# Loading two 1 KB vectors as rows and spreading one of them with four small matmuls, in place of 256 packets of 8 bytes

## The chip, the cores and the metric

One core of one Trainium2 chip. The metric is device time in microseconds (us). A profiled execution also has a span, some 2 us shorter than that time; all times inside an execution are counted from the start of its span. In the lines of the profiles PE is TensorE (PEld its weight loads), DVE is VectorE, ACT is ScalarE, POOL is GpSimd; SPq and ACTq are the instruction queues of SyncE and ScalarE, q1 is the DMA queue of the big loads and q10 that of x and gate_w.

## The reference

One decode step: a sliding-window attention branch and a gated feed-forward branch, mixed by a scalar gate.

```python
x = A_x                                              # 1 x 1 x 512
g = sigmoid((x * gate_w).sum(-1, keepdims=True))     # gate_w: 512
a = A_ref(x, k_cache, v_cache, wq, wo)               # q = x @ wq; softmax(q k) v; @ wo
b = B_ref(x, w_gate, w_up, w_down)
return g * a + (1 - g) * b
```

The attention reads the last 4096 positions of 8 key and 8 value heads, 1 MB each. With wq, wo and the three feed-forward weights that is 30.67 MB for each run; x and gate_w are 1 KB each.

## The kernel before

All big loads stand in one queue, issued by SyncE (SP) in the order wq (two halves), 8 kn (keys), w_gate, w_up, 8 vv (values), wo (two halves), wd (three pieces). Only x and gate_w come by a second queue, issued by ScalarE (ACT). They land spread over the 128 partitions, 4 elements (8 bytes) on each, as the matmuls need x:

```python
xg = const.tile([P, 2, DC], BF16, name="xg")         # P = 128, DC = 4
nc.scalar.dma_start(xg[:, 0, :], A_x[0, 0, :].rearrange("(p c) -> p c", c=DC))
nc.scalar.dma_start(xg[:, 1, :], gate_w.rearrange("(p c) -> p c", c=DC))
dq = nc.sync
for i in range(2):
    dq.dma_start(wq_sb[:, 2 * i:2 * i + 2, :], wq_v[:, 2 * i:2 * i + 2, :])
# ... kn, w_gate, w_up, vv, wo, wd on dq; the gate (z_ps, gg) from xg ...
for k in range(4):
    for c in range(DC):
        for hb in range(2):
            nc.tensor.matmul(q_ps[:, hb, :], lhsT=xg[:, 0, c:c + 1].to_broadcast([P, P]), rhs=wq_sb[:, c, ...], ...)
    nc.scalar.copy(q_sb[...], q_ps[...])
    nc.vector.transpose(qtT[...], q_sb[...])
# ... kT = transposes of kn, S_ps = scores, e_sb, pv_ps, o_ps, oY ...
for c in range(NC_O):
    nc.tensor.matmul(a_ps[q0:q0 + 32, :], lhsT=oY[:, c:c + 1].to_broadcast([P, 32]), rhs=wo_sb[:, c, :], ...)
for j in range(N_BULK):
    nc.tensor.matmul(a_ps[q0:q0 + 32, :], lhsT=hT[:, j, :], rhs=wd_sb[:, j, :], ...)
# ... f_ps with the last pieces of wd, res, store ...
```

Of the kernel before, what the change touches and what calls it, by code (L numbers as in the profile page):

```python
# [10 lines left out]
ALU = mybir.AluOpType  # L11
AX = mybir.AxisListType
BF16 = mybir.dt.bfloat16
F32 = mybir.dt.float32
# [3 lines left out]
def kernel(  # L18
# [14 lines left out]
    nc = tc.nc  # L33

    P = 128
    D = A_x.shape[-1]
    DC = D // P
# [20 lines left out]
    const = ctx.enter_context(tc.tile_pool(name="const", bufs=1))  # L58
# [4 lines left out]
    work = ctx.enter_context(tc.tile_pool(name="work", bufs=1))  # L63
    ps_big = ctx.enter_context(tc.tile_pool(name="ps_big", bufs=2, space=bass.MemoryType.PSUM))
    ps_S = ctx.enter_context(tc.tile_pool(name="ps_S", bufs=1, space=bass.MemoryType.PSUM))
    ps_m = ctx.enter_context(tc.tile_pool(name="ps_m", bufs=2, space=bass.MemoryType.PSUM))


    xg = const.tile([P, 2, DC], BF16, name="xg")
    nc.scalar.dma_start(xg[:, 0, :], A_x[0, 0, :].rearrange("(p c) -> p c", c=DC))  # L70
    nc.scalar.dma_start(xg[:, 1, :], gate_w.rearrange("(p c) -> p c", c=DC))

    dq = nc.sync
    wq_sb = big.tile([P, DC, HQ * DH], BF16, name="wq_sb", tag="big")
# [34 lines left out]
    ident = const.tile([P, P], BF16, name="ident")  # L109
# [4 lines left out]
    ones_f = const.tile([P, P], F32, name="ones_f")  # L114
# [7 lines left out]
    nc.vector.tensor_reduce(selI[:], identf[:].rearrange("p (x r) -> p r x", x=4), axis=AX.X, op=ALU.add)  # L122


    gpr = work.tile([P, DC], F32, name="gpr")
    gsum = work.tile([P, 1], F32, name="gsum")
    nc.vector.tensor_tensor(gpr[:], xg[:, 0, :], xg[:, 1, :], op=ALU.mult)  # L127
    nc.vector.tensor_reduce(gsum[:], gpr[:], axis=AX.X, op=ALU.add)  # L128
    z_ps = ps_m.tile([P, 1], F32, name="z_ps", tag="m")
    nc.tensor.matmul(z_ps[:], lhsT=ones_f[:], rhs=gsum[:], start=True, stop=True)  # L130
    gex = work.tile([P, 1], F32, name="gex")
    nc.scalar.activation(gex[:], z_ps[:], AF.Exp, scale=-1.0)
    nc.vector.tensor_scalar_add(gex[:], gex[:], 1.0)
# [7 lines left out]
    for k in range(4):  # L141
        q_ps = ps_big.tile([P, 2, 512], F32, name="q_ps", tag="b")
        for c in range(DC):
            for hb in range(2):
                n0 = k * 1024 + hb * 512
                nc.tensor.matmul(q_ps[:, hb, :], lhsT=xg[:, 0, c:c + 1].to_broadcast([P, P]),  # L146
                                 rhs=wq_sb[:, c, n0:n0 + 512], start=(c == 0), stop=(c == DC - 1))
        nc.scalar.copy(q_sb[:, k * 1024:(k + 1) * 1024], q_ps[:].rearrange("p a b -> p (a b)"))  # L148
        nc.vector.transpose(qtT[:].bitcast(F32)[:, k * 512:(k + 1) * 512],  # L149
                            q_sb[:].bitcast(F32)[:, k * 512:(k + 1) * 512])  # L150
# [13 lines left out]
    for g in range(Hkv):  # L164
# [3 lines left out]
        for dhi in range(2):  # L168
            for t in range(2):
                for hb in range(2):  # L170
                    nc.tensor.matmul(S_ps[:, hb, :], lhsT=q_st[:, g, dhi, :, t],  # L171
                                     rhs=k_v[:, hb * 16:(hb + 1) * 16, dhi, :, t],
                                     start=(g == 0 and dhi == 0 and t == 0),
                                     stop=(g == Hkv - 1 and dhi == 1 and t == 1))
# [11 lines left out]
                     start=True, stop=True)  # L186
# [11 lines left out]
    for c in range(DC):  # L198
        for j in range(4):
            for w, wsb in enumerate((wg_sb, wu_sb)):  # L200
                nc.tensor.matmul(gu_ps[32 * j:32 * j + 32, w, 0:FQ],  # L201
                                 lhsT=xg[:, 0, c:c + 1].to_broadcast([P, 32]),
                                 rhs=wsb[:, c, j * FQ:(j + 1) * FQ], start=(c == 0), stop=(c == DC - 1))


# [25 lines left out]
    for b in range(2):  # L231
        pv_ps = ps_big.tile([P, 4, P], F32, name="pv_ps", tag="b")
        for gq in range(4):
            g = 4 * b + gq
            for m in range(KB // 4):
# [3 lines left out]
                                 lhsT=eT[:, g, 4 * m:4 * m + wj, :].rearrange("p k h -> p (k h)"),  # L239
                                 rhs=vv[g][:, 4 * m:4 * m + 4, :],  # L240
                                 start=(m == 0), stop=(m == KB // 4 - 1), skip_group_check=True)
# [3 lines left out]
        for j in range(4):  # L245
            nc.tensor.matmul(o_ps[:], lhsT=pv_sb[:, j, :], rhs=sel_v[:, j, :, :],  # L246
                             start=(j == 0), stop=(j == 3))
# [11 lines left out]
    for c in range(NC_O):  # L259
        q0 = 32 * (c % 4)  # L260
        nc.tensor.matmul(a_ps[q0:q0 + 32, :], lhsT=oY[:, c:c + 1].to_broadcast([P, 32]),  # L261
                         rhs=wo_sb[:, c, :], start=(c < 4), stop=False, skip_group_check=True)
    for j in range(N_BULK):
        q0 = 32 * (j % 4)
        nc.tensor.matmul(a_ps[q0:q0 + 32, :], lhsT=hT[:, j, :], rhs=wd_sb[:, j, :],  # L265
                         start=False, stop=(j >= N_BULK - 4), skip_group_check=True)
# [14 lines left out]
    for n in range(4):  # L281
        nc.tensor.matmul(f_ps[32 * n:32 * n + 32, :], lhsT=w32[:], rhs=a_sb[:, n * P:(n + 1) * P],  # L282
                         start=False, stop=False, skip_group_check=True)
# [35 lines left out]
```

## Time and profile before

| | before |
|---|---|
| time | 84.33 us (84.29 to 84.5, 3 runs) |
| span of the profiled run | 82.5 us |
| TensorE, VectorE busy | 47.4 us, 34.4 us |
| moved from memory | 30.67 MB |
| packets on the queue of x and gate_w | 288, of which 256 carry 8 bytes |
| x, gate_w: issue to landing | 7.6 us, 12.8 us |

The lines stand in the prediction below. The DMA row of the time strip says how full the transfer engines are; the chain of waits says what ended last, link by link, but not how much slack a link has.

### The profile page before, as it was taken

The numbers are of one execution on the slowest core, as the hardware profiler recorded it, in microseconds if no ns is written. First come the engines' busy times: TensorE is split into PE (matmuls) and PEld (weight loads), VectorE is DVE, ScalarE is ACT, GpSimd is POOL, SyncE is SP. The second block draws the span as 40 slices with busy tenths as digits, with TensorE's granted clock in tenths as the row PEclk, the third lists the DMA queues.
The fourth block names the chain that finished last, engine by engine and source line by source line (L and its number), as shares of the span: only waits on it lengthen the run. The fifth ranks groups of instructions, "written<-read, shape, count | busy, mean of one in ns | idle before, by whom it ended". The sixth has DMA issues, their size and how long they took to land.

```text
span 82.5 us, 734 instructions
## 1 busy us (share of the span) xinstructions
PE 47.4 (58%) x286; PEld 20.8 (25%) x286; DVE 34.4 (42%) x43; ACT 8.9 (11%) x13; POOL 5.0 (6%) x11
## 2 busy tenths in 40 slices
PE   0000000999980059999999213999969955035950
PEld 0000000433420023444443012434354342011420
DVE  0000001300899999999990706219990011000210
ACT  1400000004463000000000060020020020000010
POOL 7970000000000000000000000000000000000000
PEclk9999999999999956999999995558999999555555
DMA  5799899999999999999999999999999999998000
GB/s 103 278 381 429 342 374 405 421 429 425 433 413 425 417 425 436 417 438 445 431 379 417 413 413 433 417 417 421 421 461 397 461 413 429 388 403 314 24 0 1
DMA packets 3898, 30.71 MB, mean 372 GB/s; under 512 B 696, under 2 KB 824, under 8 KB 952
## 3 DMA queue, kind: packets, MB, share of 16 engines
q1 hardware_dynamic: 3608, 30.67, 90.1%
q10 hardware_dynamic: 288, 0.00, 0.2%
q8 instruction: 2, 0.03, 0.2%
HBM read 30.67 MB, written 0.00 MB: 372 GB/s over the span
## 4 chain that ended last, share of the span: by engine, by line
DMA 69%; DVE 14%; PE 9%; ACT 2%; issue 1%; ACTq 0%; DVEq 0%
DMA wd_sb<-in_B_w_down_dram 30%; DMA vv<-in_A_v_cache_dram 23%; DMA xg<-in_gate_w_dram 16%; DVE kT L166 8%; PE q_ps L146 6%; ACT q_sb L148 2%; DVE qtT L149 2%; DVE qbig L158 2%; PE a_ps L265 2%; PE f_ps L282 1%; PE z_ps L130 1%; DVE a_sb L268 1%; ACTq L70 0%; DVE res L287 0%; DVE gpr L127 0%
## 5 line engine op out<-in xcount | busy, mean ns | idle before, releaser
L171 PE MATMUL S_ps<-kT,qbig 128*128 128x512 bf16 x64 | 15.4, 401 | 5.5 <-DVE qbig L158 5.5
L166 DVE STREAM_TRANSPOSE kT<-kn 128x2048 f32<-128x2048 f32 x8 | 17.8, 2276 | 0.0
L238 PE MATMUL pv_ps<-vv,eT 128*16 128x512 bf16 (+1 forms) x64 | 10.2, 408 | 0.0
L171 PEld LDWEIGHTS <-qbig 128*128 128x128 bf16 x64 | 6.4, 101 | 14.4 <-issue 7.8
L146 PE MATMUL q_ps<-wq_sb,xg 128*128 128x512 bf16 x32 | 9.2, 451 | 0.2 <-ACT q_sb L148 0.2
L130 PE MATMUL z_ps<-gsum,ones_f 128*128 128x1 f32 x2 | 0.6, 347 | 14.6 <-DVE gsum L128 14.6
L127 DVE TENSOR_TENSOR gpr<-xg 128x4 f32<-128x4 bf16 x1 | 0.2, 163 | 14.1 <-DMA xg<-in_gate_w_dram 14.1
L238 PEld LDWEIGHTS <-eT 128*16 128x16 bf16 (+1 forms) x64 | 4.1, 97 | 5.5 <-issue 1.9
L261 PE MATMUL a_ps<-wo_sb,oY 128*32 128x512 bf16 x32 | 2.9, 504 | 4.1 <-DMA wo_sb<-in_A_wo_dram 3.8
L146 PEld LDWEIGHTS <-xg 128*128 128x128 bf16 x32 | 3.7, 119 | 5.4 <-issue 3.0
L149 DVE STREAM_TRANSPOSE qtT<-q_sb 128x512 f32<-128x512 f32 x4 | 2.8, 690 | 4.8 <-ACT q_sb L148 4.8
L148 ACT CAST q_sb<-q_ps 128x1024 bf16<-128x1024 f32 x4 | 4.0, 1013 | 6.1 <-PE q_ps L146 6.1
L268 DVE COPY a_sb<-a_ps 128x256 f32<-128x256 f32 x1 | 0.4, 425 | 9.2 <-PE a_ps L265 9.2
L130 PEld LDWEIGHTS z_ps<-gsum,ones_f 128*128 128x128 f32 x2 | 0.5, 310 | 14.5 <-issue 14.5
L120 POOL MEMSET qbig<- 128x4160 bf16 x1 | 3.6, 3567 | 0.0
L201 PE MATMUL gu_ps<-wu_sb,xg 128*32 128x448 bf16 x16 | 3.2, 580 | 0.0
L201 PE MATMUL gu_ps<-wg_sb,xg 128*32 128x448 bf16 x16 | 3.2, 561 | 0.0
L219 DVE RECIPROCAL sg<-sge 128x448 f32<-128x448 f32 x1 | 3.0, 2953 | 0.0
L246 PE MATMUL o_ps<-identf,pv_sb 128*128 128x16 f32 x16 | 2.1, 265 | 1.4 <-ACT pv_sb L243 1.4
L248 DVE TENSOR_TENSOR oT<-o_ps,rb 128x16 bf16<-128x16 f32 x2 | 0.3, 169 | 6.0 <-PE o_ps L246 6.0
L188 ACT ACTIVATE nb<-mb_ps 128x1 f32<-128x1 f32 x1 | 0.2, 171 | 22.5 <-PE mb_ps L185 22.5
L246 PEld LDWEIGHTS o_ps<-identf,pv_sb 128*128 128x128 f32 x16 | 1.9, 191 | 2.4 <-ACT pv_sb L243 2.4
(52 smaller groups left out, 27.3 us busy)
## 6 DMA issues: line engine op xcount, KB each, us to landing
kn<-in_A_k_cache_dram SPq DMA_DIRECT2D x8, 1024.0 KB, 17.9
vv<-in_A_v_cache_dram SPq DMA_DIRECT2D x8, 1024.0 KB, 20.1
wq_sb<-in_A_wq_dram SPq DMA_DIRECT2D x2, 2048.0 KB, 7.5
wo_sb<-in_A_wo_dram SPq DMA_DIRECT2D x2, 2048.0 KB, 24.2
wg_sb<-in_B_w_gate_dram SPq DMA_DIRECT2D x1, 1792.0 KB, 21.7
wu_sb<-in_B_w_up_dram SPq DMA_DIRECT2D x1, 1792.0 KB, 23.6
wd_sb<-in_B_w_down_dram SPq DMA_DIRECT2D x1, 1152.0 KB, 25.1
wd_sb<-in_B_w_down_dram SPq DMA_DIRECT2D x1, 512.0 KB, 23.9
```

The costliest lines, as they stand in the source:

```text
L120: nc.gpsimd.memset(qbig[:], 0.0)
L130: nc.tensor.matmul(z_ps[:], lhsT=ones_f[:], rhs=gsum[:], start=True, stop=True)
L146: nc.tensor.matmul(q_ps[:, hb, :], lhsT=xg[:, 0, c:c + 1].to_broadcast([P, P]), rhs=wq_sb[:, c, n0:n0 + 512], start=(c == 0), stop=(c == D ...
L148: nc.scalar.copy(q_sb[:, k * 1024:(k + 1) * 1024], q_ps[:].rearrange("p a b -> p (a b)"))
L149: nc.vector.transpose(qtT[:].bitcast(F32)[:, k * 512:(k + 1) * 512], q_sb[:].bitcast(F32)[:, k * 512:(k + 1) * 512])
L166: nc.vector.transpose(kT[:].bitcast(F32), kn[g][:].rearrange("p k d -> p (k d)").bitcast(F32))
L171: nc.tensor.matmul(S_ps[:, hb, :], lhsT=q_st[:, g, dhi, :, t], rhs=k_v[:, hb * 16:(hb + 1) * 16, dhi, :, t], start=(g == 0 and dhi == 0 an ...
L201: nc.tensor.matmul(gu_ps[32 * j:32 * j + 32, w, 0:FQ], lhsT=xg[:, 0, c:c + 1].to_broadcast([P, 32]), rhs=wsb[:, c, j * FQ:(j + 1) * FQ], s ...
L219: nc.vector.reciprocal(sg[:], sge[:])
L238: nc.tensor.matmul(pv_ps[32 * gq:32 * gq + mm, :, :], lhsT=eT[:, g, 4 * m:4 * m + wj, :].rearrange("p k h -> p (k h)"), rhs=vv[g][:, 4 * m ...
L246: nc.tensor.matmul(o_ps[:], lhsT=pv_sb[:, j, :], rhs=sel_v[:, j, :, :], start=(j == 0), stop=(j == 3))
L261: nc.tensor.matmul(a_ps[q0:q0 + 32, :], lhsT=oY[:, c:c + 1].to_broadcast([P, 32]), rhs=wo_sb[:, c, :], start=(c < 4), stop=False, skip_gro ...
```

## The change

The intent: the first matmul waited for x and gate_w until 14 us. As one row each on one partition they are one data packet each. TensorE then turns x into a column: four matmuls with one row of x as weights and the number 1 as the moving operand. The gate's sum needs no spreading any more.

```diff
-    xg = const.tile([P, 2, DC], BF16, name="xg")
-    nc.scalar.dma_start(xg[:, 0, :], A_x[0, 0, :].rearrange("(p c) -> p c", c=DC))
-    nc.scalar.dma_start(xg[:, 1, :], gate_w.rearrange("(p c) -> p c", c=DC))
+    xr = const.tile([1, 2, D], BF16, name="xr")
+    nc.scalar.dma_start(xr[:, 0, :], A_x[0, :, :])
+    nc.scalar.dma_start(xr[:, 1, :], gate_w.rearrange("(o n) -> o n", o=1))
@@
-    gpr = work.tile([P, DC], F32, name="gpr")
-    gsum = work.tile([P, 1], F32, name="gsum")
-    nc.vector.tensor_tensor(gpr[:], xg[:, 0, :], xg[:, 1, :], op=ALU.mult)
+    xt_ps = ps_m.tile([P, DC], F32, name="xt_ps", tag="m")
+    for c in range(DC):
+        nc.tensor.matmul(xt_ps[:, c:c + 1], lhsT=xr[:, 0, c:D:DC], rhs=ident[0:1, 0:1],
+                         start=True, stop=True, skip_group_check=True)
+    xT = const.tile([P, DC], BF16, name="xT")
+    nc.vector.tensor_copy(xT[:], xt_ps[:])
+    gpr = work.tile([1, D], F32, name="gpr")
+    gsum = work.tile([1, 1], F32, name="gsum")
+    nc.vector.tensor_tensor(gpr[:], xr[:, 0, :], xr[:, 1, :], op=ALU.mult)
@@
-    nc.tensor.matmul(z_ps[:], lhsT=ones_f[:], rhs=gsum[:], start=True, stop=True)
+    nc.tensor.matmul(z_ps[:], lhsT=ones_f[0:1, :], rhs=gsum[:], start=True, stop=True)
@@ in the q and the feed-forward matmuls
-    lhsT=xg[:, 0, c:c + 1].to_broadcast(...)
+    lhsT=xT[:, c:c + 1].to_broadcast(...)
```

More of the change, by code (lines that the diff above doesn't have):

```diff
@@ L145 @@
                 n0 = k * 1024 + hb * 512
-                nc.tensor.matmul(q_ps[:, hb, :], lhsT=xg[:, 0, c:c + 1].to_broadcast([P, P]),
+                nc.tensor.matmul(q_ps[:, hb, :], lhsT=xT[:, c:c + 1].to_broadcast([P, P]),
                                  rhs=wq_sb[:, c, n0:n0 + 512], start=(c == 0), stop=(c == DC - 1))
@@ L201 @@
                 nc.tensor.matmul(gu_ps[32 * j:32 * j + 32, w, 0:FQ],
-                                 lhsT=xg[:, 0, c:c + 1].to_broadcast([P, 32]),
+                                 lhsT=xT[:, c:c + 1].to_broadcast([P, 32]),
                                  rhs=wsb[:, c, j * FQ:(j + 1) * FQ], start=(c == 0), stop=(c == DC - 1))
```

## The prediction

> **What bounds the kernel now.** I read the page's time strip first, then the chain of waits, the DMA queues (whole span and by stretch), the timeline of the opening, and the waits of the tail. All times are in us from the start of the profiled span, 82.5 us; the measured 84.33 us is that span and 1.8 us that no change in the kernel touches.
>
> The time strip comes first because it puts a ceiling on everything else:
>
> ```profile
> PE   0000000999980059999999213999969955035950
> DVE  0000001300899999999990706219990011000210
> DMA  5799899999999999999999999999999999998000
> GB/s 103 278 381 429 342 374 405 421 429 425 433 413 425 417 425 436 417 438 445 431 379 417 413 413 433 417 417 421 421 461 397 461 413 429 388 403 314 24 0 1
> ```
>
> A slice is 2.06 us. TensorE starts only in slice 7, but the DMA row is full from slice 2 to slice 36, while no compute engine is full throughout. The bytes are fixed at 30.67 MB. So the question is not when TensorE starts but whether the DMA engines finish earlier.
>
> The chain of waits seems to say the opposite:
>
> ```profile
> 1.16 12.82 DMA xg<-in_gate_w_dram
> ...
> 15.13 4.55 PE q_ps L146 x12
> ...
> 29.89 2.32 DVE kT L166
> 32.21 0.02 issue
> 32.23 18.95 DMA vv<-in_A_v_cache_dram
> 51.18 0.02 issue
> 51.20 25.08 DMA wd_sb<-in_B_w_down_dram
> 76.28 0.04 issue
> 76.32 1.45 PE a_ps L265 x9
> ```
>
> It puts the 12.82 us load of gate_w on the path that ended last. But the link from kT to vv is only the moment at which a vv load could be issued; it landed 18.95 us later because other loads stood before it in the same queue. At 422 GB/s, 18.95 us is 8.0 MB of queue. A link with so much work queued behind it can move several us earlier without the DMA engines noticing. The last link that pays is wd landing at 76.28 us; after that come 6.2 us of matmuls, copies and the output store, which the change does not touch.
>
> Then the queue by stretch. The DMA share and GB/s are the last two columns:
>
> ```profile
> 3.00:9.00 6.00, 0.00 (x0) 0.00 (x0) 0.00 (x0) 0.00 (x0) 2.59 (x3) 1.00 1.01 415
> 9.00:14.00 5.00, 0.00 (x0) 0.00 (x0) 0.00 (x0) 0.00 (x0) 0.00 (x0) 1.00 0.92 362
> 14.00:20.00 6.00, 5.42 (x17) 2.36 (x18) 1.07 (x6) 0.46 (x2) 0.00 (x0) 1.00 1.01 426
> 20.00:74.00 54.00, 37.59 (x226) 16.73 (x228) 32.57 (x35) 6.75 (x10) 0.00 (x0) 0.87 1.01 422
> ```
>
> From 14 to 74 us the rate is 422 to 426 GB/s at a share of 1.01: nothing starves the queue, although vv loads are issued late. Only the stretch 9 to 14 us is short, and it is a stretch with small packets in it. For 3 to 9 us the queues read:
>
> ```profile
> DMA packets 336, 2.49 MB, mean 415 GB/s; under 512 B 184, under 2 KB 184, under 8 KB 184
> q1 hardware_dynamic: 168, 2.49, 99.8%
> q10 hardware_dynamic: 168, 0.00, 1.5%
> ```
>
> The two queues alternate exactly: 168 packets of wq (q1) and 168 small ones (q10, the loads of x and gate_w).
>
> **What the Trainium skill says.** (1) "DMA: Bandwidth & Descriptors", section "Queues, rings and completion order": each DMA engine goes round-robin between its queues at packet granularity. The trace agrees, 168 to 168. (2) Same page, section "Rules for kernel authors": a [1, N] tile may fan out as 16 larger descriptors where a [128, N/128] tile makes 128 small ones, and it says which is faster has not been measured. The trace before shows the second form alone. (3) Same page, "Specifications": under 512 B a transfer is not at line rate, because of a read-modify-write. In the trace the small packets take little by themselves: 1.5% of 16 engines for 6 us is 1.44 us over 168 packets, 9 ns each. Their cost to x is the wait for a turn; their cost to the stream can only be what lies between packets. (4) "TensorE: Matmul & The Clock Gate", Part 1: the clock is halved until TensorE has been busy for some 3.4 us. The trace shows 0.43 us from one q_ps matmul to the next at first (12 in the 4.55 us piece of the chain and the few just before it), and a granted clock of 0.50 from 74 us on.
>
> **The change part by part.**
>
> *Loads.* 256 small packets go: per engine 8 for x, 8 for gate_w, and 1 semaphore packet for each. Each waits for one 16 KB packet of wq, some 0.61 us (2.49 MB / 168 packets gives 14.8 KB; 16 engines x 6 us / 168 = 0.57 us, and 16,384 B at 422/16 GB/s = 0.62 us). The first goes at about 2.9 us, so x should land at 2.9 + 9 x 0.6 = 8.3 and gate_w at 13.7: the trace has 0.74 + 7.6 = 8.3 and 1.16 + 12.8 = 14.0. With one data packet and one semaphore packet in place of nine, on one engine or on all, x lands at about 3.6 to 4.2 and gate_w at 4.8 to 5.5.
>
> *Added work before TensorE.* ident is ready at 4.91 + 0.29 = 5.20, behind the 3.57 us fill of qbig on GpSimd; four one-column matmuls take some 0.5 us. VectorE now has its two gate operations on one partition with 512 elements instead of 128 with 4. From rows of the trace (128x448 scalar operation 0.39, 128x1024 reduce 1.23) I estimate 0.6 us each instead of 0.16. They stand before selI (0.36) and the copy of xT (0.2) in VectorE's order: 5.5 + 0.6 + 0.6 + 0.4 + 0.2 = xT at about 6.5 to 7.3. That is before wq's first half lands (0.74 + 7.5 = 8.2), so all the added work is hidden.
>
> *Where q moves.* The program's order runs 8 matmuls of wq's first half, then those of its second. From 8.2 us the 8 take 3.4 us, to 11.6; then TensorE waits for the second half of wq, 4.19 MB of the stream, at 12.5 to 13.3 us. The first q_sb cast, which started at 19.71, needs 4 more matmuls: about 14.3 to 15.0. The compute chain therefore moves 4 to 5 us earlier, not 9: S_ps from 29.86 to about 25.5, pv from 54.06 to about 50.
>
> *Where that is lost.* The kT transposes then run against the landing of kn, pv against that of vv, and the output projection waits for wo as before (a_ps waited 3.77 us until 73.51). The vv loads are issued earlier into a queue that is already full. The gain of 4 to 5 us on compute is worth zero at the end.
>
> *What remains.* The queue itself. Between 3 and 14 us the engines moved 4.30 MB at 391 GB/s; at the later 423 that takes 10.2 us instead of 11. So at most 0.8 us were lost there, 0.15 of it the small packets' own time (287 x 9 ns / 16). A second count: 16 wq packets per engine at 0.62 us are 9.9 us; from 1.75 us, plus some 0.7 us that the cold first packets took longer, they would end at 12.3; they end at about 13.1. What I cannot see is whether the small packets cause it all: 3 to 9 us has as many per us as 9 to 14, and yet no loss at 415 GB/s. I count on 0.5 of the 0.8 us.
>
> Sum: 84.33 - 0.5 (queue) - 0 (compute chain) + 0 (added matmuls) = 83.8 us, a ratio of 0.994.
>
> **The rivals.** *The chain counts in full:* removing 8 to 9 us of waiting for gate_w brings 4 us or more at the end, 80 us or less. For it: the chain names that load for 15.5% of the span. Against: a DMA share of 1.01 from 14 to 74 us. The bytes alone, 30.67 MB at 425 GB/s, take 72.2 us; with 1.75 to the first packet and the 6.2 us tail that is 80.1 us of span, so 4 us off isn't there to have. *Nothing:* the loss at 9 to 14 us belongs to something else (the change from wq to kn, or how far ahead the packets are fetched), and only 0.15 us comes back: 84.2. For it: the even rate of 3 to 9 us. *A new wait:* each row goes through one engine that then trails the others, or the compute that now runs earlier disturbs the stream, or the transposes through TensorE wait long for ident: 84.5 or more. Against: 2 KB is 0.08 us of one engine, and there is slack of 1 us before wq's first half lands.
>
> **Range and chances.** The middle is the half-way case, 83.8. The low end, 83.2, is the whole 0.8 us of the queue and some 0.3 us at the start where descriptors for 256 small packets are no longer made beside those of wq. The high end, 84.4, is nothing gained and the usual scatter (84.29 to 84.5 before). Faster by over 2% needs 82.64 us or less, 1.7 us, twice what I find in the queue: 0.04. Slower by over 2% would need a wait that nothing here shows: 0.01. Within 2%: 0.95.
>
> **What would show it.** Right: x and gate_w land before 6 us; q_ps starts at about 8 us, with a wait for wq in its middle; S_ps starts at 25 to 26; a stretch 9 to 14 us nearer 420 GB/s; wd lands 0.3 to 0.8 us earlier, with the tail after it still 6.2 us; the wait of a_ps for wo as long as before or longer. Wrong: a DMA share that falls below 0.95 anywhere from 14 to 74 us, or a rate at 9 to 14 us that stays near 362 (then the rival "nothing" holds), or a tail of another length.

## The result, and the profile after

The changed kernel takes 83.66 us (83.52 to 83.77, 4 runs) against 84.41 us (84.29 to 84.5, 4 runs) for the kernel before: 0.75 us less, ratio 0.9911 with a 95% interval of 0.989 to 0.9933. A ratio here is the mean time of one kernel's fast runs over that of the other's of the same rounds, so it is not quite the ratio of the medians.

The DMA rows of the time strip of the changed kernel, slices of 2.04 us:

```profile
DMA  5799989999999999999999999999999999997000
GB/s 97 289 386 449 449 385 429 421 425 421 425 417 417 425 417 428 442 449 414 390 411 425 421 421 413 425 417 425 425 421 461 433 393 449 381 403 309 22 0 1
```

The transfer engines are as full as before, and it is slices 4 to 6 that moved more: 449, 385 and 429 GB/s where they had 342, 374 and 405. The same by stretch (last two columns: DMA share and GB/s):

```profile
3.00:9.00 6.00, 1.06 (x7) 0.80 (x7) 1.70 (x4) 0.17 (x1) 2.60 (x3) 1.00 1.03 437
9.00:14.00 5.00, 4.32 (x13) 1.55 (x12) 0.47 (x3) 0.00 (x0) 0.00 (x0) 1.00 0.96 411
14.00:20.00 6.00, 4.50 (x21) 1.75 (x18) 4.70 (x5) 3.95 (x4) 0.00 (x0) 1.00 1.01 423
20.00:74.00 54.00, 38.84 (x215) 16.68 (x216) 27.83 (x31) 3.09 (x6) 0.00 (x0) 0.78 1.01 422
```

From 14 us on nothing changed. Before it, (437 - 415) x 6 us and (411 - 362) x 5 us are 377 KB more, 0.89 us at 423 GB/s. The chain of waits of the changed kernel shows where that arrives (start, duration, what):

```profile
1.20 11.75 DMA wq_sb<-in_A_wq_dram
12.95 0.04 issue
12.99 1.04 PE q_ps L154 x4
...
26.57 23.74 DMA vv<-in_A_v_cache_dram
50.32 0.02 issue
50.33 25.14 DMA wd_sb<-in_B_w_down_dram
75.47 0.04 issue
75.51 1.45 PE a_ps L273 x9
```

The load of gate_w has left the chain, 15.5% of the span, and in its place stands wq itself, until 12.95. The vv load that follows is now in flight for 23.74 us instead of 18.95: issued 5.66 us earlier, landed 0.87 us earlier. wd lands at 75.47 instead of 76.28, 0.81 us earlier, and the tail after it is 6.2 us as before. The opening of the changed kernel, from its timeline (start, duration, engine, line, operation, what ended the idle time):

```profile
2.02 0.11 PEld L127 LDWEIGHTS <-xr 1*128 1x128 bf16 x1 [2.02 <-DMA xr<-in_A_x_dram]
...
5.25 0.26 PE L127 MATMUL xt_ps<-ident,xr 1*128 1x1 bf16 x4 [5.25 <-POOL ident L110]
...
6.76 0.68 DVE L135 TENSOR_TENSOR gpr<-xr 1x512 f32<-1x512 bf16 x1 [6.76 <-DMA xr<-in_gate_w_dram]
...
8.36 0.14 DVE L130 CAST xT<-xt_ps 128x4 bf16<-128x4 f32 x1
...
8.72 3.60 PE L154 MATMUL q_ps<-wq_sb,xT 128*128 128x512 bf16 x8
```

x was there at 2.0 us at the latest, gate_w at 6.76. The copy of xT stands behind the two gate operations in VectorE's order, so q_ps starts at 8.72, half a us after the first half of wq could have been there.

So 0.8 us came out of the first 14 us of the stream. The open question is why: is it the compute that starts 6 us earlier, the number of small packets, or something about these packets in particular?

### The profile page after: what moved, and what is told of

It is laid out like the page before. It is cut to its first block, busy times and chain, and to the rows that moved or that the text cites. A ratio compares the mean times of both kernels' runs of the same rounds, so it can differ in the third digit from the quotient of the medians.

```text
span 81.7 us, 741 instructions
## 1 busy us (share of the span) xinstructions
PE 52.4 (64%) x290; PEld 22.3 (27%) x290; DVE 35.4 (43%) x44; ACT 8.9 (11%) x13; POOL 5.0 (6%) x11
## 4 chain that ended last, share of the span: by engine, by line
DMA 74%; DVE 13%; PE 4%; ACT 2%; issue 1%; SPq 0%; DVEq 0%
DMA wd_sb<-in_B_w_down_dram 31%; DMA vv<-in_A_v_cache_dram 29%; DMA wq_sb<-in_A_wq_dram 14%; DVE kT L174 8%; ACT q_sb L156 2%; DVE qtT L157 2%; DVE qbig L166 2%; PE a_ps L273 2%; PE f_ps L290 1%; PE q_ps L154 1%; DVE a_sb L276 1%; SPq L77 0%; DVE res L295 0%; PE f_ps L283 0%; DVEq L166 0%
## 5 line engine op out<-in xcount | busy, mean ns | idle before, releaser
L179 PE MATMUL S_ps<-kT,qbig 128*128 128x512 bf16 x64 | 17.0, 433 | 5.4 <-DVE qbig L166 5.4
L246 PE MATMUL pv_ps<-vv,eT 128*16 128x512 bf16 (+1 forms) x64 | 12.2, 436 | 0.8 <-DVE h_sb L229 0.4
L154 PE MATMUL q_ps<-wq_sb,xT 128*128 128x512 bf16 x32 | 9.1, 442 | 0.9 <-DMA wq_sb<-in_A_wq_dram 0.7
L269 PE MATMUL a_ps<-wo_sb,oY 128*32 128x512 bf16 x32 | 3.8, 625 | 3.7 <-DMA wo_sb<-in_A_wo_dram 3.7
L154 PEld LDWEIGHTS <-xT 128*128 128x128 bf16 x32 | 3.4, 110 | 6.1 <-issue 3.6
L135 DVE TENSOR_TENSOR gpr<-xr 1x512 f32<-1x512 bf16 x1 | 0.7, 680 | 6.8 <-DMA xr<-in_gate_w_dram 6.8
L209 PE MATMUL gu_ps<-wu_sb,xT 128*32 128x448 bf16 x16 | 3.2, 579 | 0.0
L209 PE MATMUL gu_ps<-wg_sb,xT 128*32 128x448 bf16 x16 | 3.2, 562 | 0.0
L269 PEld LDWEIGHTS <-oY 128*32 128x32 bf16 x32 | 1.2, 128 | 6.1 <-issue 5.0
L186 DVE TENSOR_REDUCE pm<-S_ps 128x1 f32<-128x1024 f32 x1 | 1.2, 1224 | 3.7 <-PE S_ps L179 3.7
```

The source lines that it names most:

```text
L154: nc.tensor.matmul(q_ps[:, hb, :], lhsT=xT[:, c:c + 1].to_broadcast([P, P]), rhs=wq_sb[:, c, n0:n0 + 512], start=(c == 0), stop=(c == DC - 1))
L179: nc.tensor.matmul(S_ps[:, hb, :], lhsT=q_st[:, g, dhi, :, t], rhs=k_v[:, hb * 16:(hb + 1) * 16, dhi, :, t], start=(g == 0 and dhi == 0 an ...
L209: nc.tensor.matmul(gu_ps[32 * j:32 * j + 32, w, 0:FQ], lhsT=xT[:, c:c + 1].to_broadcast([P, 32]), rhs=wsb[:, c, j * FQ:(j + 1) * FQ], star ...
L246: nc.tensor.matmul(pv_ps[32 * gq:32 * gq + mm, :, :], lhsT=eT[:, g, 4 * m:4 * m + wj, :].rearrange("p k h -> p (k h)"), rhs=vv[g][:, 4 * m ...
```

## The experiments

Each run adds something to the changed kernel, and its output is correct. "Dead" loads go into a tile that nobody reads. They were taken in several rounds, on different chips, so ratios, each to the kernel before in its own round, compare better than times. Besides these I read when the first matmul on wd starts, from the one trace of each run: it waits for the load, so it shows the queue and not the clock of TensorE, which blurs the times. "Slow wq packets" counts, among the 16 KB packets of wq after the first two of each engine (224 of 256), those that took more than 0.672 us in the trace; in the changed kernel the middle one takes 0.611.

| run | dead small packets of 8 bytes | time, us | ratio | first wd matmul | slow wq packets |
|---|---|---|---|---|---|
| before | - | 84.41 | 1 | 76.32 | 46 |
| changed | - | 83.66 | 0.9911 | 75.51 | 0 |
| d0_row | none; one dead row | 83.58 | 0.990 | 75.48 | 0 |
| hold_kn0 | none; q held back | 83.76 | 0.992 | 75.43 | 0 |
| d256 | 256, scattered over wq | 83.59 | 0.9903 | 75.55 | 0 |
| two256 | 2 x 128, scattered over wq | 83.49 | 0.9901 | 75.46 | 0 |
| d512 | 512, scattered over wq | 83.74 | 0.9914 | 75.66 | 1 |
| mid256 | 256, scattered, issued at 20 us | 83.72 | 0.9915 | 75.54 | 1 |
| wqrow256 | 2 x 128, each from 1 KB of wq | 83.81 | 0.9941 | 75.95 | 11 |
| gate256 | 2 x 128, both from gate_w | 84.04 | 0.9966 | 75.91 | 33 |
| same256 | 128 of x, 128 of gate_w | 84.11 | 0.9965 | 76.22 | 36 |
| oldfirst | the same, ahead of the rows | 84.15 | 0.9942 | 76.27 | 45 |
| first256 | 256, scattered, ahead of the rows | 82.94 | 0.9819 | 75.41 | 1 |
| warm | none; 21 dead matmuls late | 82.81 | 0.9823 | 75.41 | 0 |

### Chain or stream: d256, d0_row, hold_kn0

My theory ("stream") was that each small packet costs the stream a fixed time. The rival ("chain") was the earlier compute.

```diff
 d256, behind the two row loads:
+    dead = const.tile([P, 2, DC], BF16, name="dead")
+    nc.scalar.dma_start(dead[:], A_wq.rearrange("(p c) n -> p c n", c=DC)[:, 0:2, 0:DC])
 d0_row, at the same place:
+    dead = const.tile([1, D], BF16, name="dead")
+    nc.scalar.dma_start(dead[:], A_x[0, :, :])
 hold_kn0:
-    nc.vector.tensor_copy(xT[:], xt_ps[:])
+    nc.vector.scalar_tensor_tensor(xT[:], kn[0][:, 0, 0:DC], 0.0, xt_ps[:], op0=ALU.mult, op1=ALU.add)
```

> The changed kernel with its early compute kept, plus one load that nobody reads and that brings back 256 packets of 8 bytes (and 16 semaphore packets) on the queue of x and gate_w, behind the two rows. Theory 'stream' (the small packets cost the wq stream some 46 ns of an engine each: 0.82 us x 16 engines / 284 packets): the whole gain goes, 84.3 to 84.5 us, ratio to before 0.998 to 1.002, while q_ps still starts near 8.7 us and S_ps near 24.1; the rate from 9 to 14 us falls to about 360 GB/s. Theory 'chain' (the gain is the compute that starts earlier): the gain stays, 83.6 to 83.7, ratio 0.991.

> Control: the changed kernel plus one unread load of a single row of 1 KB, at the same place in the same queue. It takes the same semaphore, and so shifts which earlier load each later load waits for, but adds only some two packets. Stream and chain both expect no change, 83.6 to 83.75 us, ratio 0.990 to 0.992. If a shift of those waits were the cost in the run with 256 packets, it would show here as well: 84.0 or more.

> The changed kernel without small packets, but the copy that makes xT also reads a piece of the first kn tile (times zero), so q_ps cannot start before that tile lands: about 15.5 to 16.0 us, later than the 14.99 of the kernel before. Stream: the gain stays, 83.6 to 83.75 us, ratio 0.990 to 0.992. Chain: the gain goes, 84.4 or more, ratio 1.000 or above.

Three lines of hold_kn0's chain of waits:

```profile
1.65 13.79 DMA kn<-in_A_k_cache_dram
...
15.75 3.36 PE q_ps L154 x8
...
75.43 1.44 PE a_ps L273 x9
```

hold_kn0 starts q_ps at 15.75 us, later than the kernel before (14.99), and S_ps at 28.9, and still takes 83.76 us, with wd as early as in the changed kernel. So the earlier compute is worth nothing: "chain" falls. d0_row says that the control changes nothing. But d256 refutes the stream theory too: 256 small packets are back in the same queue, alternating with wq's, and the time is 83.59, as in the control. The number of small packets is not the cost by itself.

### Number and place: d512, mid256

```diff
 d512: as d256, with a tile of [P, 4, DC] and [:, 0:4, 0:DC]
 mid256, after the q loop:
+    dead = const.tile([P, 2, DC], BF16, name="dead")
+    nc.scalar.copy(dead[:, 0, :], q_sb[:, HQ * DH - DC:HQ * DH])
+    nc.scalar.dma_start(dead[:], A_wq.rearrange("(p c) n -> p c n", c=DC)[:, 0:2, 0:DC])
```

> 512 unread packets of 8 bytes from the wq tensor behind the rows. If a small packet costs only the 9 ns that the trace shows for it: 33 per engine, 0.3 us, 83.9 us. If the loss has a threshold of number or of time: 84.4 us or more.

> The changed kernel plus 256 unread packets of 8 bytes, issued only after the last q_sb cast, at about 20 us, into the kn stream of 8 KB packets. 17 packets per engine, one per 0.31 us, so the stretch is about 21 to 27 us. If a small packet costs the stream the same wherever it lies (46 ns): 84.3 to 84.5 us and a rate near 365 GB/s for some 5 us. If the loss belongs to the opening of the stream alone, or to 16 KB packets: only the packets' own 9 ns, 0.15 us: 83.75 to 83.9, with the rate above 410 throughout.

d512 takes 83.74 us and mid256 83.72, some 0.15 above the control; the rate in mid256 stays at 416 GB/s from 20 to 30 us. That is no more than the packets' own time (mid256: 272 x 9 ns / 16 = 0.15 us; d512: 0.3), and within the scatter. For packets scattered over wq, neither a number up to 512 nor the place in the stream matters. Packets like those of x and gate_w were not tried later in the stream.

### Where the packets read from: same256, oldfirst, first256, two256

```diff
 same256, behind the rows (oldfirst: the same ahead of them):
+    dead = const.tile([P, 2, DC], BF16, name="dead")
+    nc.scalar.dma_start(dead[:, 0, :], A_x[0, 0, :].rearrange("(p c) -> p c", c=DC))
+    nc.scalar.dma_start(dead[:, 1, :], gate_w.rearrange("(p c) -> p c", c=DC))
 first256: the dead load of d256, ahead of the rows
 two256, behind the rows:
+    wq_d = A_wq.rearrange("(p c) n -> p c n", c=DC)
+    for i in range(2):
+        nc.scalar.dma_start(dead[:, i, :], wq_d[:, i, 0:DC])
```

> The run with 256 unread packets kept the gain; there they came from the big wq tensor and behind the rows. Here they are the very two loads of the kernel before (x and gate_w, 128 packets of 8 bytes from 1 KB each), unread, behind the two rows. Theory 'hot source' (16 engines reading one 1 KB tensor in 8-byte pieces slow the other reads): wq packets of 0.7 to 0.9 us appear, and 84.2 to 84.4 us, ratio 0.998 to 1.001. Theory 'opening' (what matters is that the small loads come first, while the queues start) or 'issue' (the moment at which the fifth and later kn loads are issued): 83.6 to 83.75 us, ratio 0.991.

> The two old loads of x and gate_w, unread, ahead of the two rows: order, source and packets of the kernel before. Both 'hot source' and 'opening' expect the loss back, 84.2 to 84.45 us. If it stays at 83.6 to 83.75 us, the loss belongs to neither, but to when the SP queue issues the later kn loads, which hangs on the semaphores of the loads before and differs here from the kernel before.

> 256 unread packets from the wq tensor, now ahead of the two rows in their queue, so that they start with wq as in the kernel before; the compute chain is late too, since the rows land behind them. Theory 'opening': the loss is back, 84.2 to 84.4 us. Theory 'hot source': 83.6 to 83.75 us.

same256 brings the loss back: wd's first matmul at 76.22, 0.71 of the 0.81 us. oldfirst, which repeats order and source of the kernel before, has it at 76.27, all but 0.05 us. The times give back less: same256's ratio of 0.9965 is some 0.45 of the 0.75 us, below the 84.2 to 84.4 us expected, and oldfirst's median is 84.15, with one of its six runs at 83.14. (Times can differ where the stream doesn't, see the last experiment; whether that is the reason in the untraced runs isn't known.) first256, with scattered packets ahead of the rows, has wd at 75.41: coming first is not the cause.

The small packets are recorded as short as in d256; the wq packets beside them got longer, and fewer were under way. same256, the queues from 8 to 12 us:

```profile
DMA packets 189, 1.56 MB, mean 389 GB/s; under 512 B 94, under 2 KB 94, under 8 KB 94
q1 hardware_dynamic: 95, 1.56, 97.2%
q10 hardware_dynamic: 94, 0.00, 1.2%
```

The same view of the kernel before:

```profile
DMA packets 174, 1.43 MB, mean 357 GB/s; under 512 B 87, under 2 KB 87, under 8 KB 87
q1 hardware_dynamic: 87, 1.43, 92.0%
q10 hardware_dynamic: 87, 0.00, 1.1%
```

In the kernel before, 92.0% of 16 engines for 4 us over 87 packets is 0.677 us per wq packet (single ones up to 0.927), where 0.611 is normal; and the shares add up to 93%, so the engines also stood idle between packets. The idle time is as large a part: two256, below, puts 106 wq packets into these 4 us, 19 more, which is 19 x 0.611 / 16 = 0.73 us; the longer packets are 87 x 0.066 / 16 = 0.36 of it. So the column of slow packets shows which runs lose, not how much. The scattered loads have neither longer packets nor gaps. But all runs with a loss had two small loads, and d256 had one. two256 separates that:

> Two unread loads of 128 packets of 8 bytes, as in the runs that lost time, but both scattered over the rows of wq (32 KB apart), as in the run with one load of 256 that lost nothing. If what costs is that all packets of a load come from the same 1 KB: 83.55 to 83.7 us, ratio 0.990 to 0.9915, and hardly a wq packet above 0.67 us between 4 and 12 us. If what costs is two loads, the change from one to the next: 83.8 us or more, ratio 0.994 or above, and slow wq packets from 9 or 10 us on.

two256 from 8 to 12 us:

```profile
DMA packets 212, 1.74 MB, mean 434 GB/s; under 512 B 106, under 2 KB 106, under 8 KB 106
q1 hardware_dynamic: 106, 1.74, 101.2%
q10 hardware_dynamic: 106, 0.00, 1.5%
```

More small packets than in same256 or before, exactly one for each wq packet, and no loss: 101.2% x 64 / 106 is 0.611 us per wq packet. The time is 83.49 us. Two loads in a row are not the cause; what is left is where the packets of a load read from.

### Which source: wqrow256, gate256

```diff
 wqrow256, behind the rows:
+    nc.scalar.dma_start(dead[:, 0, :], A_wq[0, 0:D].rearrange("(p c) -> p c", c=DC))
+    nc.scalar.dma_start(dead[:, 1, :], A_wq[1, 0:D].rearrange("(p c) -> p c", c=DC))
 gate256: both dead loads from gate_w
```

> The unread small loads again behind the two rows, with the shape and the two DMAs of x and gate_w, but each from 1 KB of a row of wq. If the loss comes from 16 engines reading one 1 KB stretch in 8-byte pieces, wherever it lies: 84.05 to 84.2 us, ratio 0.996, as with x and gate_w. If it hangs on where x and gate_w lie in the memory (on which other reads are under way there): 83.6 to 83.75 us, ratio 0.991. Two DMAs in place of one are then excluded as a cause too.

> gate_w twice in small packets (256), unread, behind the rows. In the kernel before the wq packets slow down at 8 to 11 us, when x is through and gate_w begins. If gate_w alone does it: a loss of 0.5 us or more, 84.1 to 84.4, with slow wq packets from some 5 us on. If x is needed, or the change from one to the other: 83.6 to 83.8.

wqrow256 lies between: 0.44 us of the stream is lost (75.95 against 75.51), 83.81 us. wqrow256 and two256 differ only in which addresses of wq the small packets read, so reading one 1 KB stretch per load in 8-byte pieces costs something in wq too. gate256 loses 0.40 us of stream; but 28 of its 33 slow packets begin after 10 us, none at 5 us as I had expected of gate_w alone. So each of these two accounts for about half of the 0.81 us. Why x with gate_w costs 0.7, why the slow packets come in spells (in the kernel before 10 of 46 between 4.4 and 5.3 us, the rest from 8.1 on), and what happens between the memory and the engines, stays open; spacings between 8 bytes and 32 KB were not tried.

### The fast run that nobody ordered: first256 and warm

first256 was to show a loss or nothing; it is 0.7 us faster than the changed kernel, in a wide spread (82.52 to 83.76; the slowest is sorted as a slow run by its distance alone, and counts in the median but not in the ratio). Its stream is as in d256. What differs is the clock that TensorE was granted in the tail (1.00 is full speed, 0.50 half). Stretches 70 to 75 and 75 to 80.5 us, first numbers TensorE busy, third from the end the granted clock. The changed kernel:

```profile
70.00:75.00 5.00, 1.90 (x16) 0.64 (x16) 0.00 (x0) 0.00 (x0) 0.00 (x0) 0.50 0.95 390
75.00:80.50 5.50, 3.06 (x37) 1.31 (x36) 0.72 (x2) 0.37 (x1) 0.00 (x0) 0.50 0.05 18
```

first256:

```profile
70.00:75.00 5.00, 3.15 (x41) 1.85 (x42) 0.58 (x3) 0.14 (x1) 0.00 (x0) 1.00 0.96 390
75.00:80.50 5.50, 1.72 (x37) 0.89 (x36) 0.72 (x2) 0.37 (x1) 0.00 (x0) 1.00 0.04 12
```

The same 37 matmuls of the tail take 1.72 us of TensorE instead of 3.06. In first256 the rows landed late, so the compute ran late (q_ps from 15.9 us), and more matmuls stood right before the tail (41 against 16 from 70 to 75 us). Its clock was low for a while shortly before (0.58 on average from 63.4 to 67.4 us), but was back at 1.00 from 67.4 us and stayed there through the tail. Late compute alone is no sure way to that: hold_kn0 has q_ps at the same time and a clock of 0.50 in the tail. If the clock is the reason, dead matmuls in the gaps must do the same for the changed kernel:

```diff
+    def fill(n, w, r):
+        for _ in range(n):
+            nc.tensor.matmul(S_ps[:, 0, :], lhsT=w, rhs=r, start=True, stop=True)
@@ after the second pv_sb copy is asked for / after oT / in the middle of the wo matmuls / before those of wd
+            fill(3, ident[:], vv[7][:, 28:32, :])
+    fill(3, oT[:, 16:17].to_broadcast([P, P]), vv[7][:, 28:32, :])
+            fill(10, oY[:, 0:1].to_broadcast([P, P]), wo_sb[:, 15, :])
+    fill(5, oY[:, 0:1].to_broadcast([P, P]), wo_sb[:, 31, :])
```

(S_ps is dead by then. Most of the dead matmuls read an operand that is ready only at that point, so that they cannot run earlier.)

> The run with small packets in front of the rows was faster than either kernel (82.5 to 83.8 us) while its compute was late: its trace shows a granted clock of 1.0 through the tail, where all others show 0.5. Here the changed kernel gets 21 unread matmuls in the gaps of TensorE from 64 us on, into a dead PSUM bank, so that its clock stays up. If the clock is what made that run fast: 82.5 to 82.9 us, ratio 0.978 to 0.983, clock 1.0 after 74 us. If the late compute itself did it: 83.6 or more, and up to 85 if the filling holds up the output projection.

warm, the same stretches:

```profile
70.00:75.00 5.00, 3.35 (x26) 1.33 (x26) 0.00 (x0) 0.00 (x0) 0.00 (x0) 1.00 0.95 388
75.00:80.50 5.50, 1.72 (x37) 0.90 (x36) 0.72 (x2) 0.37 (x1) 0.00 (x0) 0.91 0.05 20
```

The 0.91 is a mean: the clock is 1.00 up to 78 us, when the last matmuls are done. The run takes 82.81 us (82.6 to 82.88), ratio 0.9823 with an interval of 0.9811 to 0.9836: faster than both kernels, with a narrow spread. In its profiled run the copy of the result starts at 77.64 us instead of 78.66, while wd is no earlier than in the other runs without loss. The tail's clock is worth about as much as the change itself: 0.9911 - 0.9823, some 0.74 us.

## Why the prediction was right

The time, 83.66 us, is 0.14 us below the 83.8 predicted and inside the range. By its own steps:

- *The queue bounds the kernel, and the chain's link to gate_w has slack.* Right, and shown by hold_kn0: with q_ps as late as before, the gain stays. The share from 14 to 74 us stayed at 1.01.
- *Loads.* x was earlier than estimated (2.0 us at the latest, not 3.6 to 4.2), gate_w later (6.76, not 4.8 to 5.5). That the two queues take turns was right for the old loads; for single packets the estimate was off by up to 2 us.
- *Added work is hidden.* Nearly: xT came at 8.5 us (8.36 and 0.14) instead of 6.5 to 7.3, because gate_w was late and stands before it in VectorE's order. q_ps began at 8.72 rather than 8.2. It costs nothing, since TensorE then waits for the second half of wq until 12.99, which was predicted for 12.5 to 13.3. The four small matmuls took 0.26 us together.
- *Where q moves.* Right in kind: S_ps at 24.12, 5.7 us earlier instead of 4 to 5, because the matmuls after 12.99 ran at some 0.24 us each (1.89 us for 8) rather than at 0.43. That the rest is lost at wo and wd was right: a_ps waited for wo 3.7 us in all, as before.
- *What remains: 0.5 of the 0.8 us.* This term was mis-sized. The stream gave back 0.81 us by the landing of wd, and the time 0.75. I had held back because 3 to 9 us showed no loss at 415 GB/s; without the loads that stretch does 437, so there was a loss there as well, hidden by a wrong yardstick. (The second count was read short, too: in the trace the engines' last wq packets end at 13.25 us on average, not 13.1, and at 12.42 in the changed kernel.) The 0.5 was a half-way guess, and that it came within 0.14 us shows no insight into the cause.
- *The low end's 0.3 us at the start.* Not there: the first wq packet starts at 1.75 us in both kernels.
- *The tail.* 6.2 us, as predicted.

The cause that I gave for that term was wrong in part. The 9 ns recorded for a small packet hold, and the one-for-one turns of the two queues too. But "their cost to the stream can only be what lies between packets" failed: the wq packets themselves got longer, 0.677 instead of 0.611 us from 8 to 12 us, besides the gaps. And small packets as such are not what costs: 256 from scattered addresses cost next to nothing. Where all packets of a load read one 1 KB stretch, 0.40 to 0.44 us of the stream went, and 0.71 with x and gate_w themselves; the difference, and why such reads hold up the others, is not explained. My expectation of 46 ns for each small packet, after the result, was refuted by d256.

## What to carry to other kernels

Where the DMA row is full, count what the transfer engines lose, not what the chain names: a load can stand on the chain for 12.8 us and be worth 0.8. A tiny vector spread over 128 partitions by small packets was cheap in itself here, but it landed packet by packet behind a busy stream and held up the stream's own packets; a row and a small matmul avoided both. And when a kernel ends in a few dependent matmuls behind a wait, look at the clock granted there: filling TensorE's gaps with dead matmuls was worth some 0.74 us here.

## What the Trainium skill lacked or had wrong

- "DMA: Bandwidth & Descriptors", section "Rules for kernel authors", says of a [1, N] tile against a [128, N/128] tile that it isn't measured which is faster. Here, beside a full stream, rows of 1 KB landed at 2.0 us (at the latest) and 6.8 us, the 128 pieces at 8.3 and 14.0; the kernel's ratio is 0.9911. The rows, which nothing in this kernel splits, were not fanned out over the engines: the two loads make 4 packets in all on their queue.
- No page that I read says that 8-byte reads from one 1 KB stretch slow other reads: wq packets of 16 KB took up to 0.927 us instead of 0.611, 46 of 224 beyond 0.672, against at most 1 with scattered sources. With 1 KB stretches of wq the stream lost 0.44 us.
- "TensorE: Matmul & The Clock Gate", Part 1, has the clock fall after an idle window of some 3.4 us. In the kernel before it fell from 0.99 to 0.50 at about 70.2 us although matmuls were busy for 2.14 of the 3.40 us ahead of that, and the last of them had ended only some 0.4 us earlier. The busy time alone doesn't decide either: with dead matmuls the clock stayed at 1.00 after stretches of 3.4 us with 2.97 and 3.10 us of matmuls, but also after one with 1.93 (70.8 to 74.2 us). What does decide stays open.
